# The first layer of chunks 4 to 11 taken in pairs of chunks, as seven block products in place of eight

## The chip, the cores and the metric

The kernel runs on one core of a Trainium2 chip. The metric is the device time of one launch in microseconds, the median over runs. TensorE (PE) multiplies, VectorE (DVE) and ScalarE (ACT) work on its results, GpSimd (POOL) on data outside PSUM, SyncE (SP) issues most transfers.

## What is computed

Attention with a local window, eight global keys and a distance bias, then a two-layer network with a Gelu:

```python
scores = scale * np.matmul(q, k.transpose(0, 1, 3, 2)) + bias
scores = np.where(keep, scores, -1000000000.0)
a = np.exp(scores - np.max(scores, axis=-1, keepdims=True))
a = a / (np.sum(a, axis=-1, keepdims=True) + 1e-09)
x = np.matmul(a, v)            # 4 batches, 8 heads, 768 tokens, 64 -> 3072 tokens x 512
h = x @ w_in                   # 512 -> 2048
g = 0.5 * h * (1.0 + erf(h / np.sqrt(2)))
out = g @ w_out                # 2048 -> 512
```

## The kernel before

The 3072 tokens are cut into 12 chunks of 256 (`CT`). A chunk's attention is taken by head pairs `p` = 0 to 3: `scores_pair` (PE, then a masked maximum on DVE, L373), `exps` (exponentials on ACT, L402; factors on DVE, L404 and L405; scaling on POOL, L411), `flip` (transposes on PE, L423, and a copy on ACT, L427), `av_pair` (products with the values for two head pairs at once, L461; the two partial sums are copied by ACT, L493, and added by DVE, L494; then x is split into two float16 parts, the high one by ACT, L496, the low one by DVE, L191).

Every float32 operand of the network is split into a high and a low float16 part, and a product is three matmuls: high by high, high by low, low by high. The hidden 2048 columns are taken in 8 steps of 256. In a step of a chunk `m1` computes both 128-column halves of the hidden layer (`f` = 0, 1: 12 matmuls of 256 columns each, L537) into one PSUM tile `h`; `gelu` runs the Gelu on ACT (L553) and splits it on DVE (L554, L192); `m2` adds the step to the chunk's two output tiles `acc` (`k` = 0, 1: 6 matmuls of 512 columns each, L581). `send` copies a finished tile on ACT, sends it, and DVE takes its row maxima.

`run` writes the order out by hand as a loop over a time T, one step each: first layer of step T+1, its Gelu, second layer of step T, and between them the pieces of attention that `att` finds due. `START` gives the T at which a chunk's attention begins and `EVENTS` the offsets of its pieces. Chunk c's attention (c at least 3) begins at T = 8c - 7, takes 8 steps, and its scores and exponentials come two head pairs at a time (`EVS`). A compiler then places the instructions, each engine works its own queue in order, and a wait in a queue holds all behind it.

The weights arrive as 64-bit words; they are turned into floats (`split_weights`, L233 to L237) and split (`part_weights`, L247, L192) during the first steps, in which chunks 0 and 1 go side by side. From T = 19 on the words are loaded a second time and compared (`check_load`, `check_words`, L261, 32 pieces of four DVE operations), every second step. `bounds` keeps running maxima and minima of x and of the weights on DVE (L196).

ACT holds one table at a time; between exponentials and Gelus it loads another (ACT_TABLE_LOAD). `self.table` fixes the order of the two kinds.

## Time and profile before

| | |
|---|---|
| median of 3 runs | 647.58 us (647.2 to 648.36) |
| profiled execution | 647.65 us, its span 645.8 us |
| PE busy | 628.7 us, 97% of the span |
| DVE busy | 369.2 us, 57% |
| ACT busy | 313.0 us, 48% |
| POOL busy | 80.4 us, 12% |
| mean granted clock of PE | 0.991 |

The span reaches from the first to the last instruction that the profile shows; the time of the execution is 1.85 us longer. A busy share is an average over stages. Which engine the end hangs on is read stage by stage, from the stretches and from what each waits for. Lengths of operations that follow each other on one engine overlap; the distance of their starts is what one costs.

### The profile page before, as it was taken

What the parts mean: (1) busy time and instruction counts of PE and PEld (TensorE: products, weight loads), DVE (VectorE), ACT (ScalarE), POOL (GpSimd) and SP (SyncE); (2) the same over time, 40 slices, a digit from 0 to 9 for tenths busy, and PEclk for the clock granted to TensorE, in tenths of its full rate; (3) what the DMA queues carried; (4) which work ended last, traced back from release to release, by engine and by line L of the source; (5) the groups of instructions that cost most, each with busy time, mean ns of one, the idle gap of its engine ahead of it and who ended that gap; (6) DMA issues with size and microseconds to landing.
All of it is one profiled execution on the core that took longest, in us unless ns stands there. A gap on an engine that the chain in (4) does not pass through costs nothing.

```text
span 645.8 us, 14522 instructions
## 1 busy us (share of the span) xinstructions
PE 628.7 (97%) x5712; PEld 424.3 (66%) x5712; DVE 369.2 (57%) x1160; ACT 313.0 (48%) x757; POOL 80.4 (12%) x175
## 2 busy tenths in 40 slices
...
GB/s 256 261 177 266 262 73 192 115 37 144 171 24 143 119 56 162 113 37 147 80 94 165 49 124 165 11 138 133 17 172 128 37 172 66 33 2 1 34 1 38
DMA packets 66187, 71.27 MB, mean 110 GB/s; under 512 B 32704, under 2 KB 49344, under 8 KB 66112
## 3 DMA queue, kind: packets, MB, share of 16 engines
...
q14 instruction: 28, 0.23, 0.1%
HBM read 63.97 MB, written 6.29 MB: 109 GB/s over the span
## 4 chain that ended last, share of the span: by engine, by line
PE 84%; DVE 9%; ACT 4%; issue 1%; DMA 1%; POOL 0%; POOLq 0%; ACTq 0%; DVEq 0%
PE h L537 33%; PE acc L581 32%; PE av L461 5%; PE t L423 5%; PE s L362 4%; PE h L531 2%; PE acc L566 2%; DVE wb L235 2%; ACT n L402 1%; DVE wb L237 1%; DVE wb L233 1%; DVE n L373 1%; DVE gl L192 1%; DVE ta L150 1%; DVE winl L192 1%
## 5 line engine op out<-in xcount | busy, mean ns | idle before, releaser
L537 PE MATMUL h<-x,winh 128*128 128x256 f16 x1344 | 228.3, 274 | 0.9 <-ACT x L503 0.4
L537 PE MATMUL h<-x,winl 128*128 128x256 f16 x672 | 184.0, 274 | 0.0
L554 DVE TENSOR_SCALAR gh<-gr 128x512 f16<-128x512 f32 x96 | 42.7, 445 | 213.6 <-ACT gr L553 213.6
L537 PEld LDWEIGHTS <-winh 128*128 128x128 f16 x1344 | 131.5, 98 | 32.9 <-issue 1.4
L411 POOL TENSOR_SCALAR n<-n,su 128x192 f32<-128x192 f32 (+1 forms) x160 | 75.2, 489 | 494.3 <-ACT n L402 240.2
L553 ACT ACTIVATE gr<-h 128x512 f32<-128x512 f32 x96 | 57.3, 597 | 153.9 <-issue 87.3
L581 PE MATMUL acc<-wouth,gl 128*128 128x512 f16 x336 | 127.0, 379 | 1.0 <-DVE gl L192 1.0
L581 PE MATMUL acc<-wouth,gh 128*128 128x512 f16 x336 | 127.5, 380 | 0.1
L581 PE MATMUL acc<-woutl,gh 128*128 128x512 f16 x336 | 127.3, 379 | 0.0
L581 PEld LDWEIGHTS <-gh 128*128 128x128 f16 x672 | 64.2, 98 | 66.0 <-issue 4.3
L427 ACT COPY pt<-t 128x384 f32<-128x384 f32 x96 | 45.1, 475 | 93.7 <-PE t L423 92.0
L537 PEld LDWEIGHTS <-winl 128*128 128x128 f16 x672 | 66.1, 98 | 9.7 <-issue 0.8
L192 DVE SCALAR_TENSOR_TENSOR gl<-gr,gh 128x512 f16<-128x512 f32 x96 | 66.7, 694 | 8.5
L402 ACT ACTIVATE n<-n,mn 128x192 f32<-128x192 f32 (+1 forms) x144 | 62.1, 432 | 4.1 <-DVE mn L373 3.9
L581 PEld LDWEIGHTS <-gl 128*128 128x128 f16 x336 | 32.9, 98 | 41.0 <-DVE gl L192 1.5
L373 DVE CUSTOM_DVE_ANT_0 n<-s,pens 128x192 f32<-128x192 f32 (+1 forms) x192 | 54.9, 341 | 0.1
L423 PE MATMUL t<-ident,n 128*128 128x128 f32 x288 | 47.8, 276 | 3.2 <-DVE n L411 2.4
L461 PE MATMUL av<-pt,vr 64*64 64x64 f32 (+2 forms) x1312 | 42.4, 250 | 2.0 <-ACT pt L427 2.0
L461 PEld LDWEIGHTS av<-pt,vr 64*64 64x64 f32 (+1 forms) x1312 | 35.4, 134 | 11.5 <-issue 8.0
L423 PEld LDWEIGHTS t<-ident,n 128*128 128x128 f32 x288 | 34.7, 142 | 8.5 <-DVE n L411 2.4
L362 PE MATMUL s<-kr,qr 64*64 64x192 f32 (+2 forms) x752 | 39.1, 323 | 0.7 <-DMA kr<-kT 0.7
L261 DVE SCALAR_TENSOR_TENSOR wand<-c,wand 128x128 int32<-128x128 int32 x128 | 37.5, 293 | 2.7
...
## 6 DMA issues: line engine op xcount, KB each, us to landing
...
kr<-kT SPq DMA_DIRECT2D x36, 64.0 KB, 3.3
```

The source lines that it names most:

```text
L192: return self.nc.vector.scalar_tensor_tensor(out=out, in0=in_, scalar=scale, in1=hi, op0=ALU.mult, op1=ALU.subtract)
L362: ins = nc.tensor.matmul(out, lhsT=lhs, rhs=rhs, start=True, stop=True).ins
L373: ins = nc.vector.tensor_tensor_reduce(out=nn[:, j * NK:j * NK + n], in0=sp[hh][:, j, 0:n], in1=self.pens[:, 2 * p + hh, o:o + n], scale=- ...
L402: self.table(nc.scalar.activation(out=nn, in_=nn, func=AF.Exp, bias=mn[:, i:i + 1], scale=-1.0, accum_out=su[:, i:i + 1]))
L411: ins = eng.tensor_scalar(out=nn, in0=nn, scalar1=su[:, i:i + 1], scalar2=0.0, op0=ALU.mult, op1=ALU.add)
L423: self.last_t = nc.tensor.transpose(tp[:, i, :], nn[:, o:o + P], self.ident).ins
L427: ins = nc.scalar.copy(pt, tp).ins
L461: ins = nc.tensor.matmul(out, lhsT=lhs, rhs=rhs, start=start, stop=stop, skip_group_check=True).ins
L537: ins = nc.tensor.matmul(hp[:, f, :], lhsT=w[:, d, fs], rhs=x[:, d, e, :], start=n == 0, stop=n == 3 * NP - 1).ins
L553: self.table(nc.scalar.activation(out=gr, in_=hp, func=AF.Gelu, scale=1.0 / (WS * XS)))
L554: nc.vector.tensor_scalar(out=gh, in0=gr, scalar1=GS, scalar2=None, op0=ALU.mult)
L581: ins = nc.tensor.matmul(acc, lhsT=g[:, f, ks], rhs=w[:, f, :], start=s == 0 and n == 0, stop=(s == NST - 1 or (c, s) == (NCH - 1, NST - 2 ...
```

## The change

Chunks 0 to 3 keep the loop over T, which ends after chunk 3. Chunks 4 to 11 go in four pairs. A **double** `n` (0 to 15, and a 16th pass that only finishes) takes two chunks and two steps, so the first layer is a 2 by 2 block product: weights A (two hidden steps by two halves of the 512 inputs), tokens B (two halves of the inputs by two chunks). It is computed from seven block products P1 to P7 of 12 matmuls each, in place of eight. Four of the weight blocks are replaced by the sums S1 to S4, formed once (`sums`, every second T from 19 on), four of the token blocks by the differences T1 to T4 (`tokens`, once for each pair of chunks). P1, P6, P5 and P3 pile up in one PSUM tile, `hX`; P2, and then P7 and P4, in another, `hW`, which P7 starts anew. In between ACT copies the state after P1, P6 and P7 out, and DVE adds P2, P4 and P5 to the copies. These are three of the four results C11, C21, C22; C12 is what `hX` holds at the end. Each gets its Gelu and split (`gelu2`).

`ORDER` lists what PE does in a double: the seven products, and eight times `m`, a second-layer half (6 matmuls of 512 columns) of the double before. In double 0 there is none before, so its `m` places are empty. A double also has half a chunk's attention, that of chunk 6 + n // 2, until double 11.

The attention of chunks 3, 4 and 5 begins at T = 15, 21 and 27, six steps apart, with a batch of exponentials for each head pair (`EVC`). The check of the weights moves into the doubles, as do the weights' bounds. x is kept in float32 as well (`xf`).

```diff
-START = [-7, -3, 8] + [8 * c - 7 for c in range(3, NCH)]
+START = [-7, -3, 8, 15, 21, 27]
 EVF = {"load": -9, "loadv": -9, "s": (0, 1, 2, 3), "exp": (0, 1, 2, 3), "pt": (2, 3, 4, 5), "av": (2, 3, 4, 5)}
-EVS = {"load": -3, "loadv": 1, "s": (0, 0, 4, 4), "exp": (0, 0, 4, 4), "pt": (2, 3, 6, 7),
-       "av": (4, 4, 8, 8)}
-EVT = {"load": -2, "loadv": 2, "s": (0, 1, 4, 5), "exp": (1, 1, 5, 5), "pt": (3, 4, 7, 8),
-       "av": (5, 5, 9, 9)}
-EVENTS = [EVF, EVF, EVT] + [EVS] * (NCH - 3)
+EVT = {"load": -2, "loadv": 2, "s": (0, 1, 4, 5), "exp": (1, 1, 5, 5), "pt": (3, 4, 7, 8), "av": (5, 5, 9, 9)}
+EVC = {"load": -1, "loadv": 3, "s": (0, 1, 3, 4), "exp": (0, 1, 3, 4), "pt": (2, 3, 5, 6), "av": (4, 4, 7, 7)}
+EVENTS = [EVF, EVF, EVT, EVC, EVC, EVC]
+PAIRED = 4
...
-STEPS += [(c, s) for c in range(2, NCH) for s in range(NST)]
+STEPS += [(c, s) for c in range(2, PAIRED) for s in range(NST)]
+DOUBLES = 4 * (NCH - PAIRED) // 2
+ORDER = ("P1", "m", "P2", "m", "P7", "m", "P6", "m", "P4", "m", "P5", "m", "m", "P3", "m")
+FACTORS = {"P1": ("A11", "B11"), "P2": ("A12", "B21"), "P3": ("S4", "B22"), "P4": ("A22", "T4"), "P5": ("S1", "T1"),
+           "P6": ("S2", "T2"), "P7": ("S3", "T3")}
...
-        a = self.sm.tile([P, 512], I32, name=f"wb{s}_{i}", tag="o", bufs=3)
+        a = self.sw[s][:, i] if i < 2 else self.sm.tile([P, 512], I32, name=f"wb{s}_{i}", tag="o", bufs=3)
...
-            xs = self.sm.tile([P, 2, n, P], F32, name=f"xs{c}_{p}", tag="o", bufs=3)
-            nc.scalar.copy(xs, rows[1])
-            nc.vector.tensor_tensor(out=xs, in0=rows[0], in1=xs, op=ALU.add)
-            xh, xl = (self.x[c][:, ps.start:ps.stop, e].rearrange("d p (j q) -> d j p q", j=2) for e in range(2))
-            nc.scalar.copy(xh, xs)
-            self.lo_dve(xl, xs, xh)
+            xf = self.xf[c % 2][:, ps.start:ps.stop].rearrange("d p (j q) -> d j p q", j=2)
+            t = self.sm.tile([P, 2, n, P], F32, name=f"xs{c}_{p}", tag="o", bufs=3)
+            nc.scalar.copy(t, rows[1])
+            nc.vector.tensor_tensor(out=xf, in0=rows[0], in1=t, op=ALU.add)
+            xh, xl = (self.x[c][:, ps.start:ps.stop, e] for e in range(2))
+            xf = self.xf[c % 2][:, ps.start:ps.stop]
+            nc.scalar.copy(xh, xf)
+            if c < PAIRED or c % 2 == 0 or p == NP - 1:
+                self.lo_dve(xl, xf, xh)
             if p == NP - 1:
-                self.bounds(self.xtop, self.xlow, self.x[c][:, :, 0, :])
+                self.bounds(self.x[c][:, :, 0, :])
...
+    def sums(self, s):
+        nc = self.nc
+        a = self.sw[s].bitcast(F32).rearrange("p i (d f) -> p i d f", d=2)
+        a11, a21, a12, a22 = a[:, 0, :, 0:P], a[:, 0, :, P:], a[:, 1, :, 0:P], a[:, 1, :, P:]
+        t = self.stg.tile([P, 4, 2, P], F32, name=f"sf{s}", tag="stage")
+        for o, x, y, op in ((0, a21, a22, ALU.add), (1, t[:, 0], a11, ALU.subtract), (2, a11, a21, ALU.subtract),
+                            (3, a12, t[:, 1], ALU.subtract)):
+            self.behind(nc.vector.tensor_tensor(out=t[:, o], in0=x, in1=y, op=op))
+        half = self.sw[s].rearrange("p i c -> p (i c)").bitcast(F16).rearrange("p (e c) -> p e c", e=2)
+        flat = t.rearrange("p s d f -> p (s d f)")
+        nc.scalar.activation(out=half[:, 0], in_=flat, func=AF.Copy, scale=WS)
+        self.behind(self.lo_dve(half[:, 1], flat, half[:, 0], WS))
...
+    def tokens(self, c):
+        nc = self.nc
+        xa, xb = self.xf[c % 2], self.xf[(c + 1) % 2]
+        t1 = None
+        for j, x, y in ((2, xb[:, 2:4], xb[:, 0:2]), (0, xb[:, 0:2], xa[:, 0:2]), (1, xb[:, 2:4], 0), (3, xa[:, 2:4], 1)):
+            t = self.sm.tile([P, 2, CT], F32, name=f"xt{c}_{j}", tag="o", bufs=3)
+            nc.vector.tensor_tensor(out=t, in0=x, in1=t1 if isinstance(y, int) else y, op=ALU.subtract)
+            t1 = t
+            nc.scalar.copy(self.xt[:, j, 0], t)
+            self.lo_dve(self.xt[:, j, 1], t, self.xt[:, j, 0])
...
+    def product(self, n, name):
+        nc = self.nc
+        c, u = PAIRED + 2 * (n // 4), n % 4
+        which = "X" if name in ("P1", "P6", "P5", "P3") else "W"
+        start = name in ("P1", "P2", "P7")
+        if name in ("P1", "P2"):
+            self.h[which] = self.bank([P, 2, CT], f"h{which}{n}")
+        out = self.h[which]
+        first = True
+        for i in range(2):
+            (wh, wl), (xh, xl) = (self.factor(f, c, 2 * u + i) for f in FACTORS[name])
+            for d in range(2):
+                for w, x in ((wh, xh), (wh, xl), (wl, xh)):
+                    ins = nc.tensor.matmul(out[:, i], lhsT=w[:, d], rhs=x[:, d], start=start and first,
+                                           stop=i == 1 and d == 1 and w is wl, skip_group_check=True).ins
+                    self.unit(ins, first)
+                    first = False
+        if name in ("P1", "P6", "P7"):
+            self.part[name] = self.cp.tile([P, 2, CT], F32, name=f"{name}_{n}", tag=name)
+            nc.scalar.copy(self.part[name], out)
+        elif name in ("P2", "P4", "P5"):
+            t = self.part[{"P2": "P1", "P4": "P6", "P5": "P7"}[name]]
+            nc.vector.tensor_tensor(out=t, in0=out, in1=t, op=ALU.add)
...
+    def gelu2(self, n, name):
+        nc = self.nc
+        f, j, src = {"C11": (0, 0, "P1"), "C22": (1, 1, "P7"), "C21": (1, 0, "P6"), "C12": (0, 1, None)}[name]
+        gr = self.part[src] if src else self.gp.tile([P, 2, CT], F32, name=f"gr{n}", tag="gr")
+        self.table(nc.scalar.activation(out=gr, in_=gr if src else self.h["X"], func=AF.Gelu, scale=1.0 / (WS * XS)))
+        gh, gl = (self.gp.tile([P, 2, CT], F16, name=f"g{e}{n}_{name}", tag=f"g{e}", bufs=6) for e in "hl")
+        self.behind(nc.vector.tensor_scalar(out=gh, in0=gr, scalar1=GS, scalar2=None, op0=ALU.mult))
+        self.lo_dve(gl, gr, gh, GS)
+        self.g[n, j, f] = gh, gl
...
+    def second(self, n, m):
+        nc = self.nc
+        j, k, i = m // 4, m // 2 % 2, m % 2
+        c, u = PAIRED + 2 * (n // 4) + j, n % 4
+        s = 2 * u + i
+        if s == 0:
+            pool, tag = (self.ps, "ps") if j else (self.ps_acc, "ps_acc")
+            self.acc[c, k] = pool.tile([P, DM], F32, name=f"acc{c}_{k}", tag=tag)
...
+    def pairs(self, flag_i):
+        self.last_unit = None
+        self.part = {}
+        self.cp = self.ctx.enter_context(self.tc.tile_pool(name="cp", bufs=1))
+        for n in range(DOUBLES + 1):
+            c, p = PAIRED + 2 + n // 2, 2 * (n % 2)
+            att = c < NCH
+            if n == DOUBLES:
+                self.flag(flag_i)
+            m = 0
+            for at, name in enumerate(ORDER):
+                if att:
+                    if at in (0, 3):
+                        self.scores_pair(c, p + at // 3)
+                        self.exps(c, p + at // 3)
+                    if at in (6, 7, 9, 10):
+                        self.flip(c, 2 * p + (6, 7, 9, 10).index(at))
+                    if at == 11:
+                        self.av_pair(c, p + 1)
+                if name != "m":
+                    if n < DOUBLES:
+                        self.product(n, name)
+                elif n:
+                    self.second(n - 1, m)
+                    m += 1
+                if n < DOUBLES and at in (5, 9, 11, 13):
+                    self.gelu2(n, {5: "C11", 9: "C21", 11: "C22", 13: "C12"}[at])
+                if att and p and c + 1 < NCH:
+                    if at == 6:
+                        self.load(c + 1)
+                    if at == 13:
+                        self.load_v(c + 1)
+                if n < 16 and at in (1, 8):
+                    self.check_load(2 * n + (at == 8))
+                if n < 16 and at in (8, 14):
+                    self.check_words(2 * n + (at == 14))
+                if 4 <= n < 12 and at == 12:
+                    self.bounds(self.win[n - 4][0])
+            if n % 4 == 3 and n + 1 < DOUBLES:
+                self.tokens(PAIRED + 2 * (n // 4 + 1))
...
-            k = T - 16 - GAP
-            if 0 <= k < 64 and k % 2 == 0:
-                self.check_load(k // 2)
-            if 2 <= k < 66 and k % 2 == 0:
-                self.check_words((k - 2) // 2)
             if T in (15, 16):
-                self.bounds(self.xtop, self.xlow, self.x[T - 15][:, :, 0, :])
-            if 20 <= T < 36 and T % 2 == 0:
-                self.bounds(self.wtop, self.wlow, self.win[(T - 20) // 2][0])
+                self.bounds(self.x[T - 15][:, :, 0, :])
+            if T >= 19 and T % 2:
+                self.sums((T - 19) // 2)
+            if T == 32:
+                self.load(PAIRED + 2)
...
+        self.load_v(PAIRED + 2)
+        self.tokens(PAIRED)
+        self.pairs(flag_i)
```

Three places where rows stand otherwise than before. The first is DVE where the first layer of chunk 4 begins. Before, in a step (this one is of a later chunk, all are alike), Gelu splits follow each other, with a piece of the weight check and the add of an attention sum:

```order
L554 TENSOR_SCALAR gh_4735<-gr_4737 128x512
L192 SCALAR_TENSOR_TENSOR gl_4736<-gr_4737,gh_4735 128x512
L554 TENSOR_SCALAR gh_4789<-gr_4791 128x512
L192 SCALAR_TENSOR_TENSOR gl_4790<-gr_4791,gh_4789 128x512
L261 SCALAR_TENSOR_TENSOR wand<-c_2_4698,wand 128x128 x4
L554 TENSOR_SCALAR gh_4843<-gr_4845 128x512
L192 SCALAR_TENSOR_TENSOR gl_4844<-gr_4845,gh_4843 128x512
L494 TENSOR_TENSOR xs_3_4883<-av_3_0_4849,xs_3_4883 128x512
```

Now, at double 0 (`xt` are the differences T, `P_0` the copy of P1, `s` the scores of chunk 6; ISA is the masked maximum):

```order
L756 TENSOR_REDUCE otop<-o_1_3270 128x1
L377 ISA n_0_3310,mn_0_3298<-s_0_3300,pens 128x128
L377 ISA mn_0_3298 128x1
L377 ISA n_0_3310,mn_0_3298<-s_0_3300,pens 128x192
L377 ISA mn_0_3298 128x1
L377 ISA n_1_3313,mn_0_3298<-s_1_3301,pens 128x128
L377 ISA mn_0_3298 128x1
L377 ISA n_1_3313,mn_0_3298<-s_1_3301,pens 128x192
L377 ISA mn_0_3298 128x1
L616 TENSOR_TENSOR xt_0_3283<-xf_347,xf_346 128x512
L193 TENSOR_TENSOR xt<-xt_2_3279,xt 128x512
L662 TENSOR_TENSOR P_0_3340<-hW_3344,P_0_3340 128x512
```

The add of P2, for which P7 waits, stands behind the row maximum of chunk 3's output, a head pair's four maxima, the difference T1 and the low part of T3.

The second is DVE after a chunk's attention is complete. Before, the attention sum, a head pair's maxima, the low part of x and the bounds:

```order
L494 TENSOR_TENSOR xs_3_4883<-av_3_0_4849,xs_3_4883 128x512
L373 ISA n_0_4902,mn_0_4890<-s_0_4892,pens 128x192
L373 ISA mn_0_4890 128x1
L373 ISA n_0_4902,mn_0_4890<-s_0_4892,pens 128x192
L373 ISA mn_0_4890 128x1
L373 ISA n_1_4905,mn_0_4890<-s_1_4893,pens 128x192
L373 ISA mn_0_4890 128x1
L373 ISA n_1_4905,mn_0_4890<-s_1_4893,pens 128x192
L373 ISA mn_0_4890 128x1
L191 TENSOR_TENSOR x<-xs_3_4883,x 128x2x2x128
L196 TENSOR_TENSOR xtop<-xtop,x 128x1024
L196 TENSOR_TENSOR xlow<-xlow,x 128x1024
```

Now, at double 4, where the pair of chunks changes:

```order
L377 ISA n_0_4485,mn_0_4473<-s_0_4475,pens 128x192
L377 ISA mn_0_4473 128x1
L194 SCALAR_TENSOR_TENSOR gl_C_4437<-gr_4434,gh_C_4436 128x512
L377 ISA n_1_4488,mn_0_4473<-s_1_4476,pens 128x192
L377 ISA mn_0_4473 128x1
L377 ISA n_1_4488,mn_0_4473<-s_1_4476,pens 128x192
L377 ISA mn_0_4473 128x1
L193 TENSOR_TENSOR xt<-xt_3_4469,xt 128x512
L412 TENSOR_TENSOR nmax<-nmax,mn_0_4473 128x4
L408 TENSOR_SCALAR su_0_4474<-su_0_4474 128x4
L409 RECIPROCAL su_0_4474<-su_0_4474 128x4
L662 TENSOR_TENSOR P_4_4515<-hW_4525,P_4_4515 128x512
```

The low part of the last difference and the split of the Gelu of C12 (`gl_C`) stand among the maxima of a head pair; the add of P2 follows four rows after that low part, behind the factors `su`.

The third is ACT in the steps before the pairs, a chunk's two later head pairs. Before, one load for two head pairs:

```order
L402 ACT_TABLE_LOAD
L402 ACTIVATE n_4_2695,su_2_2684<-n_4_2695,mn_2_2683 128x192 x2
L402 ACTIVATE n_5_2698,su_2_2684<-n_5_2698,mn_2_2683 128x192 x2
L402 ACTIVATE n_6_2713,su_3_2702<-n_6_2713,mn_3_2701 128x192 x2
L402 ACTIVATE n_7_2716,su_3_2702<-n_7_2716,mn_3_2701 128x192 x2
L553 ACT_TABLE_LOAD
L553 ACTIVATE gr_2793<-h_2766 128x512
L427 COPY pt_4_2832<-t_4_2828 128x384
L553 ACTIVATE gr_2848<-h_2815 128x512
```

Now a load to and from the exponentials for each, with a weight sum (`sw`) between:

```order
L406 ACT_TABLE_LOAD
L406 ACTIVATE n_4_2399,su_2_2388<-n_4_2399,mn_2_2387 128x192 x2
L406 ACTIVATE n_5_2402,su_2_2388<-n_5_2402,mn_2_2387 128x192 x2
L607 ACTIVATE sw_870<-sf_2428 128x1024
L557 ACT_TABLE_LOAD
L557 ACTIVATE gr_2462<-h_2435 128x512
L499 COPY xs_1_2500<-av_1_1_2467 128x512
L503 CAST x<-xf_346 128x2x256
L406 ACT_TABLE_LOAD
L406 ACTIVATE n_6_2517,su_3_2506<-n_6_2517,mn_3_2505 128x192 x2
L406 ACTIVATE n_7_2520,su_3_2506<-n_7_2520,mn_3_2505 128x192 x2
L431 COPY pt_4_2574<-t_4_2570 128x384
```

Here the Gelu `gr` and the second batch each stand behind a load of their own; in the whole program there are 28 and 27 loads for the two kinds, and before 22 and 21.

## Rows read from the trace of the kernel before

**Rows 1.** The page, part 1: busy us, share of the span, instructions.

```profile
PE 628.7 (97%) x5712; PEld 424.3 (66%) x5712; DVE 369.2 (57%) x1160; ACT 313.0 (48%) x757; POOL 80.4 (12%) x175
```

**Rows 2.** Busy times by stretch: us, busy of each engine, clock, DMA, GB/s.

```profile
140.00:180.00 40.00, 40.00 (x393) 27.52 (x390) 23.93 (x81) 21.98 (x56) 6.94 (x16) 1.00 0.45 143
...
580.00:620.00 40.00, 40.00 (x331) 27.27 (x329) 17.65 (x32) 7.42 (x13) 0.00 (x0) 1.00 0.04 14
```

**Rows 3.** Timeline of PE, 189 to 206 us: start, length, line, operation.

```profile
189.31 1.49 PE L461 MATMUL av<-pt,vr 64*64 64x128 f32 x45
...
192.10 0.39 PE L581 MATMUL acc<-wouth,gh 128*128 128x512 f16 x1
...
199.91 0.38 PE L537 MATMUL h<-x,winh 128*128 128x256 f16 x2
...
201.22 0.49 PE L423 MATMUL t<-ident,n 128*128 128x128 f32 x3
201.55 0.38 PE L537 MATMUL h<-x,winh 128*128 128x256 f16 x2
...
203.18 0.38 PE L581 MATMUL acc<-wouth,gh 128*128 128x512 f16 x1
...
205.77 0.38 PE L537 MATMUL h<-x,winh 128*128 128x256 f16 x2
```

**Rows 4.** Groups of DVE by shape: busy us, mean ns, idle before.

```profile
L261 DVE SCALAR_TENSOR_TENSOR wand<-c,wand 128x128 int32<-128x128 int32 x128 | 37.5, 293 | 2.7
...
L494 DVE TENSOR_TENSOR xs<-av,xs 128x512 f32<-128x512 f32 x18 | 12.4, 689 | 2.9 <-ACT xs L493 2.9
```

**Rows 5.** Timeline of DVE, 192 to 199 us.

```profile
192.60 0.69 DVE L191 TENSOR_TENSOR x<-xs,x 128x512 f16<-128x512 f32 x1 [0.68 <-ACT x L496]
193.21 0.68 DVE L196 TENSOR_TENSOR xtop<-xtop,x 128x1024 f16<-128x1024 f16 x1
...
194.42 0.35 DVE L373 CUSTOM_DVE_ANT_0 n<-s,pens 128x192 f32<-128x192 f32 x1
...
194.69 0.35 DVE L373 CUSTOM_DVE_ANT_0 n<-s,pens 128x192 f32<-128x192 f32 x1
```

**Rows 6.** Groups of ACT by shape.

```profile
L553 ACT ACTIVATE gr<-h 128x512 f32<-128x512 f32 x96 | 57.3, 597 | 153.9 <-issue 87.3 <-PE h L537 62.4 <-PE h L531 4.0
L402 ACT ACTIVATE n<-n,mn 128x192 f32<-128x192 f32 x120 | 52.8, 441 | 2.9 <-DVE mn L373 2.8
L427 ACT COPY pt<-t 128x384 f32<-128x384 f32 x96 | 45.1, 475 | 93.7 <-PE t L423 92.0 <-ACT o L608 1.6
L402 ACT ACT_TABLE_LOAD x22 | 28.2, 1283 | 7.4 <-DMA qr<-qT 7.0
L553 ACT ACT_TABLE_LOAD x21 | 26.9, 1283 | 0.8
...
L493 ACT COPY xs<-av 128x512 f32<-128x512 f32 x18 | 10.5, 586 | 13.1 <-PE av L461 13.1
```

**Rows 7.** Groups of POOL by shape.

```profile
L411 POOL TENSOR_SCALAR n<-n,su 128x192 f32<-128x192 f32 x136 | 66.9, 507 | 366.1 <-ACT n L402 240.2 <-DVE su L405 101.1 <-DVE mx L698 21.8
```

**Rows 8.** Busy times by stretch of 2 us, 48 to 56 us.

```profile
48.00:50.00 2.00, 0.23 (x2) 0.14 (x2) 1.90 (x7) 2.00 (x7) 0.00 (x0) 1.00 0.00 0
50.00:52.00 2.00, 2.00 (x16) 1.28 (x16) 2.00 (x6) 2.00 (x5) 0.00 (x0) 0.72 0.91 285
52.00:54.00 2.00, 2.00 (x11) 1.56 (x10) 2.00 (x5) 0.67 (x3) 0.00 (x0) 0.50 1.02 334
54.00:56.00 2.00, 2.00 (x47) 1.35 (x46) 1.02 (x2) 1.97 (x4) 0.00 (x0) 0.93 1.20 323
```

**Rows 9.** DMA: KB and median us to landing, then the queue's timeline at 167 us.

```profile
kr<-kT SPq DMA_DIRECT2D x36, 64.0 KB, 3.3
...
167.22 0.38 SPq L299 DMA_DIRECT2D qr<-qT  x1
167.71 5.18 SPq L299 DMA_DIRECT2D kr<-kT  x8
```

107 lines of the change are left out of this document (66 added, 41 removed).

## The prediction

> **What bounds the kernel now.** I read the page first, then the busy times by stretch, then the order of TensorE's work in a step. TensorE (PE) is busy 97% of the span, VectorE (DVE) 57%, ScalarE (ACT) 48% [rows 1]. From 140 us to 620 us PE is busy in all of each 40 us stretch; twelve stretches, of which the first and the last stand in [rows 2]. There PE's own work is the time, and a matmul taken away is time gained, if nothing else comes to make PE wait. The price is read from starts, since the recorded lengths overlap: twelve first-layer matmuls run from 199.91 to 201.22, so 1.31 us or 109 ns each; three transposes take 0.33; twelve second-layer matmuls run from 203.18 to 205.77, 2.59 us [rows 3]. A step (24 and 12 matmuls) is 5.21 us. A half of a chunk's attention costs PE 2.79 (value products 1.39, scores of two head pairs 0.7 each) [rows 3] and four groups of transposes of 0.33.
>
> **What is removed.** A double replaces 4 steps: 8 blocks of 12 matmuls become 7. Over 16 doubles 192 matmuls go, at 109 ns: **21.0 us**. Nothing else leaves PE; all attention and the second layer are only moved.
>
> **What is added off PE.** In a double ACT gets three copies out of PSUM and DVE three adds. The nearest rows are the copy of an attention sum, 0.59, and its add, 0.69 [rows 4, 6]. DVE's lengths overlap too: the 128x512 low part of x, 0.69 long, holds its queue for 0.61 from its start to the next one's, a masked maximum, 0.35 long, for 0.27 [rows 5]; I take 0.60 and 0.28 for queues. A double with attention lasts 4 x 5.21 - 1.31 + 4.1, so about 23.7 us. ACT's share of it is three copies, four Gelus at 0.60, eight exponentials at 0.44, four probability copies at 0.48, two passes of an attention block and two table loads at 1.28 [rows 6], 13.4 in all; DVE's, counted in the same way, is about 14. Both fit. So the cost lies only where PE comes to a block before what it waits for. I played the queues of the new program by hand against these starts; four places matter.
>
> (1) **A usual double.** P7 restarts the bank that P2 filled, so it waits for DVE to add P2. Between the two stand scores (0.7) and one second-layer half (1.30): 2.0 us of cover against 0.7 to 0.8 for the add and its start, 1.2 spare. The add stands behind the scale factors of the head pair, and these behind its exponentials; the exponentials end some 3.8 us after the double begins and P2 at 4.7, so the add isn't late. P4 needs ACT's copy of P7: P7 ends at 8.0, ahead of the copy are four exponentials, a load and a Gelu, it is done at 10.2, and PE comes at 12.6. P5 needs the copy of P6, 11.5 against 15.9; P3 the add of P5, 18.1 against 21.2. No wait: 0.
>
> (2) **The first double** has no second layer between its blocks, and the token differences T1 to T4 of its own chunks are formed in it. Count from the last value product of chunk 5. PE does the second layer (2.6), scores, P1, P2, scores, and stands at P7 at 6.7. DVE gets the attention sum at 0.7, waits for ACT's rounding until 2.7, and then works without a pause: the low part, two bounds, T3, a row maximum, four score maxima, T1, T3's low part, P2's add: 8 x 0.60 + 4 x 0.28 + 0.09, done at 8.7. PE waits 2.0. Twelve entries later comes T2's low part, at 13.0, and the first transposes need the factors that stand just ahead of it and then GpSimd, 0.5 for each operation [rows 7]: P6 waits 3.0. P4 waits 0.9 for ACT, which has two table loads and seven exponentials on the way to T4, and then 0.35 for its low part; a transpose 0.65. Together 6.9, and the next double, whose exponentials start late, waits 0.9 for its transposes: **7.8**. With the full lengths (0.69 in place of 0.60) the same count gives 9.6; half of it if the queues stand closer.
>
> (3) **The three later changes of pair.** The differences of the next pair stand in DVE's queue ahead of P2's add. From the add of P5 on, 17.35 after the double's start, come the two Gelu splits, the attention sum, four differences, four low parts, two bounds and four maxima. In the fifth double the add also stands behind the scale factors, whose exponentials wait for ACT to finish the differences and load a table (29.0); it ends at 32.1, PE is there at 30.5: 1.6. In the ninth, with two more bounds but ahead of the factors, 31.3: 0.9. In the thirteenth there is no attention, so only 1.3 of cover, and ten operations of the weight check at 0.29 [rows 4] crowd the queue: 32.1 against 29.0, 3.1. Together **5.6**; with full lengths 10.4.
>
> (4) **TensorE's clock.** In 48 to 50 us PE ran 0.23 of 2 us, and in the next 6 us the granted share was 0.72, 0.50 and 0.93, half speed being the 1.2 GHz level [rows 8]: 0.56 + 1.0 + 0.14, about 1.7 us of PE time lost. The wait ahead of P6 and the one in the thirteenth double are as long. I take one such fall, **1.7**, with 0 and 3.4 as bounds.
>
> **The steps before the pairs** get one more chunk's attention (moved, not added), eight weight sums and twelve more table loads (28 + 27 in place of 22 + 21). A chunk's attention now lies on six steps, for PE 6 x 5.21 + 8.2 = 39.5. ACT has four batches of exponentials with two loads each, 4 x (2 x 1.28 + 4 x 0.44) = 17.3, eight probability copies 3.8, two attention blocks 2.4, six Gelus 3.6, three sums of 1024 at most 1.2 each, 3.6, and an output, 0.8: 31.5 of 39.5. A Gelu can come 1.7 late after a load; its user comes 5.5 later and the chain to it takes 1.8. DVE has less: a sum is four adds of 256 and a split of 1024, under four and two times the 0.69 of 512 [rows 4], some 3 us in two steps. I take 0.5, up to 3, for all of it. Chunk 4's keys now have two steps (11 us and more) where three lay before; its issues took from 167.2 to 172.9 and a landing of such a piece 3.3 [rows 9], 9 in all, so 0. The tail is as it was.
>
> **The sum.** -21.0 + 7.8 + 5.6 + 1.7 + 0.5 = -5.4. The profiled execution took 647.65 (span 645.8, 1.85 around it), 0.07 above the median, 647.58. **Forecast: 642.2 us.**
>
> **Two banks for seven blocks.** In [rows 3] a block starts where the second layer ends, with no wait for an eviction; there each step has a PSUM tile of its own. The seven blocks share two tiles. If each of the five reuses in a double were exposed for a copy or add and its start, about 0.65, that would cost 16 x 3.3 = 52 us, less 21: 679. Against it stands that between a block and its tile's reuse lie 2.0 us or more of other matmuls, apart from the first and the last doubles, where the adds still fit into 1.3. The Trainium skill, Perfetto Trace Analysis, section Optimizing Tensor Performance, speaks against this change: independent groups of matmuls should rotate through different PSUM banks, so that one's eviction overlaps the next. By that rule it would be the 679, by the rows 642.2; no row of before shows a tile reused so soon.
>
> **Rivals.**
> *The queues keep up better* (what DVE waits for comes earlier than in my count; half of (2) and (3), no clock fall): 647.6 - 21.0 + 6.7 = 633. For it: DVE was idle for over a third of the span [rows 1]. Against it: in (2) the count has hardly a pause in it.
> *The usual double waits too: slower.* Its 1.2 us of cover ahead of P7 is used up, because the exponentials that stand ahead of P2's add start late: on ACT they come behind the last Gelu of the double before and a table load of 1.28. Each us beyond the 1.2 costs a us in each of eleven doubles. From 0.5 us on average (5.4 / 11) it is no faster than before; at 1.0 it gives 653. For it: ACT's queue has loads of 1.28 that can slip; against it: spare on three chains.
> *The gain is eaten without a single cause* (first double at its full lengths, two clock falls, 3 in the steps before): 642.2 + 1.8 + 1.7 + 2.5 = 648, no change. It is also what would be seen if the words of the weight check, loaded behind v, came late in the first double, since the check stands ahead of later sums on DVE.
> *Every reuse of the two banks exposed*: 679, by the reasons above the least likely.
>
> **How the numbers follow.** Forecast 0.55, better queues 0.17, the late exponentials 0.15, no change 0.10, every reuse exposed 0.03. 0.2% is 1.3 us, about what a measurement of this kernel can tell from no change: faster 0.72, same 0.10, slower 0.18. The range runs from just under the second case, 632, to the slower one at half a us to one per double, 652.
>
> **What would show it.** In the profile of after: PE's first-layer matmuls 192 fewer; PE full in the usual doubles, with no wait for DVE ahead of P7; two or three PE waits of 1 to 3 us in the first double, behind DVE's low parts and GpSimd; one of about 1 to 3 ahead of P7 in the fifth, ninth and thirteenth; the clock share down once. It is wrong if PE waits in every double, if the steps before chunk 4 get longer by more than one chunk's attention, or if the first double takes under 18 or over 27 us from the last value product of chunk 5.

## The result and the profile after

The changed kernel takes **656.62 us** (median of 4 runs, 656.35 to 657.81). Its time is 1.014 of that of the kernel before (95% interval 1.0123 to 1.0158): 1.4% slower, where 642.2 was forecast and 632 to 652 given as range. The profiled execution took 656.35, its span is 654.5 (645.8 before).

From the page, the busy times (us, share, instructions) and the stores (issues, KB each, median us to landing):

```profile
PE 625.7 (96%) x5520; PEld 406.9 (62%) x5520; DVE 432.4 (66%) x1276; ACT 371.9 (57%) x841; POOL 84.2 (13%) x173
...
out<-o ACTq DMA_DIRECT2D x23, 256.0 KB, 2.0
```

The 192 matmuls are gone (5520 in place of 5712), but PE is busy only 3 us less than in [rows 1]: what is left takes longer, so the busy time tells little. I measured each double, from the start of its P1 to the start of the next one's. The starts of doubles 2 and 3 in the timeline of PE:

```profile
305.40 0.39 PE L653 MATMUL hX<-x,winh 128*128 128x256 f16 x2
...
328.86 0.88 PE L366 MATMUL s<-kr,qr 64*64 64x192 f32 x16
329.68 0.39 PE L653 MATMUL hX<-x,winh 128*128 128x256 f16 x2
```

A usual double lasts 305.40 to 329.68, 24.3 us (24.1 to 24.3 in eight of them, 24.2 on average), a double without attention 19.5; no wait of PE stands between 282 and 350 us. Four doubles are longer, those that begin a pair of chunks: 0 (23.2, without second layer, so 13.8 of its own), 4 (26.6), 8 (26.7) and 12 (27.6 in place of 19.5). The balance against the kernel before, in us:

| | forecast | measured | from |
|---|---|---|---|
| eighth product left out, 16 doubles | -21.0 | -20.6 | 19.55 for a double without attention, 4 x 5.21 before |
| attention in usual doubles | 0 | +6.0 | 12 x (24.2 - 23.7) |
| doubles 0 and 1 | +7.8, clock 1.7 | +9.4, 0 in double 1 | 23.2 - 13.8 |
| doubles 4, 8, 12 | +1.6, +0.9, +3.1 | +2.4, +2.5, +8.1 | over 24.2, 24.2, 19.5 |
| steps before the pairs | +0.5 | +2.9 | double 0 begins at 258.1; the same work was done at 255.2 before |
| the end, behind the last second-layer matmul | 0 | -1.4 | 7.3 before, 5.9 now |

The 255.2 is worked out: the second layer of chunk 4's first step began at 253.46 before. The changed kernel has not done two first-layer steps of it (5.2) at 258.1, but has done three more blocks of scores (2.1), value products twice (2.8) and six more groups of transposes (2.0). The 23.7 fits the kernel before as well: there four steps with half a chunk's attention take 25.0 on average, less 1.31 for a block.

The table sums to 9.3. From it goes one head pair's scores, 0.8, which the usual doubles count and double 11 hasn't (it lasts 23.5): 8.5, and the spans differ by 8.7; 0.2 is not placed.

**Double 0.** The timeline of PE:

```profile
260.81 0.77 PE L366 MATMUL s<-kr,qr 64*64 64x128 f32 x16
263.58 2.69 PE L653 MATMUL hW<-xt,sw 128*128 128x256 f16 x12 [2.00 <-DVE P L662]
267.36 0.37 PE L653 MATMUL hX<-xt,sw 128*128 128x256 f16 x1 [1.08 <-ACT xt L618]
269.85 1.09 PE L427 MATMUL t<-ident,n 128*128 128x128 f32 x3 [2.12 <-POOL n L415]
```

The timeline of DVE in the same stretch:

```profile
262.85 0.69 DVE L662 TENSOR_TENSOR P<-hW,P 128x512 f32<-128x512 f32 x1
...
265.96 0.69 DVE L616 TENSOR_TENSOR xt<-xf,xt 128x512 f32<-128x512 f32 x1 [1.67 <-issue]
...
266.92 0.28 DVE L265 SCALAR_TENSOR_TENSOR wand<-c,wand 128x128 int32<-128x128 int32 x1
...
268.33 0.17 DVE L409 RECIPROCAL su<-su 128x4 f32<-128x4 f32 x1
```

The DMA issues between 250 and 270 us (count, KB each, median us to landing):

```profile
c<-w SPq DMA_DIRECT2D x3, 512.0 KB, 8.6
...
out<-o ACTq DMA_DIRECT2D x2, 256.0 KB, 6.2
```

P7 waits 2.0 for P2's add, as counted. But the third difference, T2, stands 1.7 us at the head of DVE's queue, released by no engine. Its buffer is one that outputs use too (`own_ring` below takes that away), and the two stores of chunk 3 take 6.2 us to land in place of 2.0 (page), beside 512 KB pieces of the weight check and smaller ones of v. By the trace the second store, issued at 258.12, landed at 265.88; T2 starts at 265.96. Comparisons stand between what follows, the factors of the transposes among it (268.33).

**Double 12.** The queue of SP from 480 us on:

```profile
497.96 3.03 SPq L303 DMA_DIRECT2D vr<-v  x6
501.09 48.26 SPq L204 DMA_DIRECT2D c<-w  x12
```

The timeline of DVE, 541 to 567 us:

```profile
543.09 0.94 DVE L265 SCALAR_TENSOR_TENSOR wand<-c,wand 128x128 int32<-128x128 int32 x3 [1.02 <-DMA c<-w]
543.95 0.68 DVE L662 TENSOR_TENSOR P<-hW,P 128x512 f32<-128x512 f32 x1
...
551.84 0.62 DVE L265 SCALAR_TENSOR_TENSOR wand<-c,wand 128x128 int32<-128x128 int32 x2 [0.86 <-DMA c<-w]
552.38 0.68 DVE L500 TENSOR_TENSOR xf<-av,xs 128x512 f32<-128x512 f32 x1
...
561.94 0.68 DVE L662 TENSOR_TENSOR P<-hW,P 128x512 f32<-128x512 f32 x1
```

The waits of PE, 540 to 580 us (us in total, times, longest):

```profile
PE hW L653 <- DVE P L662: 5.5, 1, 5.5
```

From 501 us on the last twelve loads of the check follow one another, as fast as their three buffers come free, and DVE compares whatever has landed. In DVE's order 34 of the 128 comparisons stand between the start of double 11 and the attention sum `xf`, where the program lists eight for a double. DVE waits at them for words that are still on the way (1.02 and 0.86), the attention sum begins at 552.38, 5.5 us after the value products end (1.0 in `no_check` below), and P2's add at 561.94: PE waits 5.5.

**Doubles 4 and 8** have the waits that were forecast, for P2's add, and one for scores. The waits of PE, 350 to 380 us:

```profile
PE hW L653 <- DVE P L662: 1.3, 1, 1.3
```

And 450 to 470 us:

```profile
PE hW L653 <- DVE P L662: 0.9, 1, 0.9
PE s L366 <- DVE mn L377: 0.4, 1, 0.4
```

These waits are 1.3 in each of the two, of the 2.4 and 2.5 that the doubles are longer. The rest is no wait that the profile shows and no fall of the clock. Part of it: the compiler cut the value products of both in two, 4 and 60 matmuls with second-layer matmuls between, and the scores of double 4 in 2 and 14. What such a cut costs is measured below.

**The clock** fell twice, in doubles 0 and 12 (busy times by stretch; the granted share stands before the last two columns, and 0.50 is the 1.2 GHz level):

```profile
262.00:264.00 2.00, 0.41 (x3) 0.31 (x3) 2.00 (x7) 1.99 (x9) 0.00 (x0) 0.91 0.98 384
264.00:266.00 2.00, 2.00 (x11) 1.44 (x10) 0.34 (x5) 1.85 (x9) 0.00 (x0) 0.50 0.55 216
...
270.00:272.00 2.00, 2.00 (x9) 1.37 (x10) 1.70 (x5) 1.17 (x3) 2.00 (x4) 0.50 0.00 0
560.00:562.00 2.00, 0.00 (x0) 0.00 (x0) 2.00 (x6) 1.11 (x2) 0.00 (x0) 0.65 0.01 4
562.00:564.00 2.00, 1.32 (x7) 0.95 (x7) 2.00 (x6) 0.63 (x1) 0.00 (x0) 0.50 0.37 139
```

### The profile page after: what moved, and what is told of

Its sections match the earlier page's. It is cut to its first block, busy times and chain, and to the rows that moved or that the text cites. A ratio compares the mean times of both kernels' runs of the same rounds, so it can differ in the third digit from the quotient of the medians.

```text
span 654.5 us, 14272 instructions
## 1 busy us (share of the span) xinstructions
PE 625.7 (96%) x5520; PEld 406.9 (62%) x5520; DVE 432.4 (66%) x1276; ACT 371.9 (57%) x841; POOL 84.2 (13%) x173
## 4 chain that ended last, share of the span: by engine, by line
PE 69%; DVE 13%; DMA 6%; ACT 5%; SPq 4%; issue 2%; POOL 0%; DVEq 0%; ACTq 0%; POOLq 0%
PE acc L688 20%; PE hX L653 11%; PE hW L653 8%; PE acc L585 8%; PE h L541 7%; SPq L303 4%; PE s L366 4%; PE av L466 4%; PE t L427 3%; DMA c<-w 3%; PE acc L570 3%; PE h L535 2%; DMA kr<-kT 2%; ACT n L406 2%; DVE xt L616 1%
## 5 line engine op out<-in xcount | busy, mean ns | idle before, releaser
L688 PE MATMUL acc<-wouth,gh_C 128*128 128x512 f16 x256 | 97.7, 382 | 0.0
L688 PE MATMUL acc<-woutl,gh_C 128*128 128x512 f16 x256 | 97.6, 381 | 0.0
L688 PE MATMUL acc<-wouth,gl_C 128*128 128x512 f16 x256 | 97.3, 380 | 0.0
L653 PEld LDWEIGHTS <-sw 128*128 128x128 f16 x768 | 76.7, 100 | 29.1 <-issue 11.2
L688 PEld LDWEIGHTS <-gh_C 128*128 128x128 f16 x512 | 48.7, 98 | 40.7 <-issue 3.7
L541 PE MATMUL h<-x,winh 128*128 128x256 f16 x320 | 55.2, 274 | 1.5 <-ACT x L511 1.4
L653 PE MATMUL hX<-xt,sw 128*128 128x256 f16 x384 | 49.1, 277 | 1.1 <-ACT xt L618 1.1
L653 PEld LDWEIGHTS <-winh 128*128 128x128 f16 x384 | 36.7, 98 | 14.8 <-issue 3.3
L466 PE MATMUL av<-pt,vr 64*64 64x128 f32 (+2 forms) x1312 | 44.3, 250 | 1.6 <-ACT pt L431 1.6
L688 PEld LDWEIGHTS <-gl_C 128*128 128x128 f16 x256 | 25.2, 98 | 30.0 <-issue 0.6
L541 PE MATMUL h<-x,winl 128*128 128x256 f16 x160 | 43.8, 274 | 0.0
```

The source lines that it names most:

```text
L466: ins = nc.tensor.matmul(out, lhsT=lhs, rhs=rhs, start=start, stop=stop, skip_group_check=True).ins
L541: ins = nc.tensor.matmul(hp[:, f, :], lhsT=w[:, d, fs], rhs=x[:, d, e, :], start=n == 0, stop=n == 3 * NP - 1).ins
L653: ins = nc.tensor.matmul(out[:, i], lhsT=w[:, d], rhs=x[:, d], start=start and first, stop=i == 1 and d == 1 and w is wl, skip_group_check ...
L688: ins = nc.tensor.matmul(acc, lhsT=g, rhs=w[:, f, :], start=s == 0 and q == 0, stop=q == 5 and s in (NST - 3, NST - 1), skip_group_check=T ...
```

## The experiments

Sixteen runs, each beside the kernel before on the same chip (medians 648.05 to 648.19; 647.72 beside the changed kernel). Doubles 0, 4, 8, 12 are from the profiled execution, us:

| run | median us | ratio (95%) | 0 | 4 | 8 | 12 |
|---|---|---|---|---|---|---|
| changed kernel | 656.62 | 1.0140 (1.0123 to 1.0158) | 23.2 | 26.6 | 26.7 | 27.6 |
| no_check | 641.77 | 0.9900 (0.9882 to 0.9918) | 20.0 | 25.0 | 24.6 | 19.8 |
| no_loads | 648.86 | 1.0034 (1.0007 to 1.0061) | 20.9 | 25.5 | 25.0 | 23.2 |
| own_ring | 653.77 | 1.0102 (1.0049 to 1.0155) | 19.4 | 25.0 | 29.4 | 27.1 |
| fill | 658.03 | 1.0139 (1.0097 to 1.0181) | 25.1 | 26.9 | 25.7 | 25.4 |
| pin_alone | 648.53 | 1.0008 (0.9986 to 1.0030) | 23.3 | 25.2 | 25.1 | 20.4 |
| check_spread | 649.54 | 1.0042 (1.0009 to 1.0074) | 18.9 | 24.8 | 26.1 | 27.0 |
| pinned | 644.58 | 0.9969 (0.9939 to 0.9999) | 18.9 | 25.9 | 26.0 | 21.0 |
| queue | 643.71 | 0.9945 (0.9912 to 0.9979) | 18.9 | 24.8 | 25.0 | 21.6 |
| queue_cover | 643.56 | 0.9959 (0.9924 to 0.9995) | 18.9 | 25.3 | 25.3 | 21.4 |
| queue_early | 641.96 | 0.9915 (0.9891 to 0.9938) | 16.8 | 25.3 | 25.3 | 21.4 |
| early_cover | 647.87 | 0.9989 (0.9964 to 1.0013) | 16.9 | 25.3 | 25.6 | 21.5 |
| pinned_early | 644.49 | 0.9948 (0.9921 to 0.9975) | 16.8 | 25.4 | 26.1 | 19.7 |
| pinned_pairs | 655.26 | 1.0101 (1.0058 to 1.0145) | 17.0 | 25.9 | 25.9 | 19.7 |
| av_next_to_scores | 658.96 | 1.0185 (1.0123 to 1.0248) | 24.5 | 25.9 | 27.7 | 28.1 |
| before_split | 653.22 | 1.0073 (1.0051 to 1.0095) | | | | |
| before_av_apart | 652.97 | 1.0075 (1.0051 to 1.0098) | | | | |

The single runs of most versions of the changed kernel scatter by 6 to 9 us. In the profiles double 0 begins at 258 to 260 us, but at 264.5 in `fill`, whose edit touches nothing there. The traces show where that comes from: the first scaling of chunk 2's exponentials on GpSimd. In the changed kernel, in the timeline of POOL:

```profile
96.88 0.91 POOL L415 TENSOR_SCALAR n<-n,su 128x192 f32<-128x192 f32 x1 [92.70 <-DVE su L409]
```

And in `fill`:

```profile
99.23 4.33 POOL L416 TENSOR_SCALAR n<-n,su 128x192 f32<-128x192 f32 x1 [95.05 <-DVE su L410]
```

It takes 4.33 in place of 0.91, PE waits 3.0 for the transposes behind it, and the granted clock is 0.50 in 106 to 108 us. Why the same operation takes so long there is open. So the doubles are compared one by one.

**The weight check.**

```
no_check: -  self.check_load(...)  -  self.check_words(...)    # both left out of the doubles
no_loads: -  w = self.raw.pop((n, "chk"))
          +  w = self.sw[0] ...        # words that lie in SBUF, result into a tile of its own
```

> The changed kernel without the second loading and the comparison of the weight words in the doubles (left out, 32 pieces; the flag then says nothing of them). Theory W (the words come late: their loads crowd the stores and the loads in double 0, and DVE stands at a comparison for words that have not landed ahead of double 12): the wait ahead of P7 in double 12 falls from 5.5 to 2 or less and TensorE's clock keeps its level there (another 2.4), the second wait of double 0 (1.1 for the low clock's P6 and 2.1 for GpSimd) falls by about 1.5; together 6 to 8, 649 to 651. Rival (the queue is long by itself, the words only fill gaps): only the ten comparisons of 0.29 ahead of the add in double 12 go, 3 us at most, 653.5 to 656.

> The changed kernel with all 128 comparisons in their places, but of words that lie in SBUF already, into a tile of their own: the second loading of the weights in the doubles is left out, and nothing is checked. Without loads and comparisons the time was 641.8. Theory W (the loads do the damage: they delay stores and hold DVE at words that have not landed): most of the 14.8 us comes back, the comparisons alone leave 1 to 4 at the changes of pair: 643 to 646. Rival V (DVE's own time does it, 128 comparisons of 0.3 are 38 us ahead of other things): 651 to 657.

Without the check the kernel takes 641.77, 14.9 less and twice what was expected, and the four doubles together are 14.7 shorter. The whole loss against the forecast has about this size, but it is not the check's alone (the last part comes back to this). In double 0 T2 then follows P2's add at once, as the timeline of DVE of `no_check` shows:

```profile
263.27 0.69 DVE L662 TENSOR_TENSOR P<-hW,P 128x512 f32<-128x512 f32 x1
...
263.94 0.68 DVE L616 TENSOR_TENSOR xt<-xf,xt 128x512 f32<-128x512 f32 x1
...
267.40 0.17 DVE L409 RECIPROCAL su<-su 128x4 f32<-128x4 f32 x1
```

And the clock keeps its level, in the busy times of `no_check` by stretch:

```profile
262.00:264.00 2.00, 0.25 (x8) 0.10 (x1) 2.00 (x7) 1.99 (x6) 0.00 (x0) 1.00 0.00 0
...
266.00:268.00 2.00, 0.59 (x6) 0.41 (x5) 1.64 (x6) 1.98 (x10) 0.23 (x1) 1.00 0.00 0
```

Comparisons without loads leave 5.2 of the 14.7 (0.9, 0.5, 0.4 and 3.4); loads and late words make the other 9.5. Both theories have a part; in the doubles the loads have the larger one. By the medians the split is even (7.1 and 7.8): the profiled execution of `no_loads` was the fastest of ten. In double 12 the comparisons alone still make PE wait, in the waits of PE of `no_loads`, 545 to 575 us:

```profile
PE hW L655 <- DVE P L664: 3.5, 1, 3.5
```

That is near the 3.1 that was forecast for double 12. And the clock keeps its level beside this wait, in the busy times of `no_loads` by stretch:

```profile
552.00:554.00 2.00, 0.00 (x0) 0.00 (x0) 2.00 (x6) 0.72 (x2) 0.00 (x0) 1.00 0.01 4
```

**A buffer of its own for T.**

```
-  name=f"xt{c}_{j}", tag="o", bufs=3
+  name=f"xt{c}_{j}", tag="xt", bufs=2
```

> The changed kernel with the token differences in two buffers of their own; before they took turns with the outputs and the attention sums in three. In double 0 the third difference, T2, stood 1.7 us on DVE with no engine named as its releaser, and went on when the stores of chunk 3, slow beside the loads, were through. Theory R (it waits for the buffer of a store): double 0 gets 1.5 to 3 us shorter (23.2 to some 21), the rest as it was: 654 to 655. Rival (it waits for something else, or what follows is late anyway): double 0 within 0.5 us of 23.2, 656.6.

Double 0 is 3.8 shorter, more than expected: the wait was for the buffer of a store. Double 8 got 2.7 longer, with a wait of 2.3 for P2's add in place of 0.9 and a fall of the clock to 0.50 that the changed kernel didn't have; why its queue stood otherwise was not tested.

**Filling the waits.**

```
+  self.fill(18 ahead of P7, 20 ahead of P6 in double 0; 45 ahead of P7 in double 12)
```

> The changed kernel with idle transposes of the identity (0.109 each) where TensorE waits: 18 ahead of P7 and 20 ahead of P6 in double 0, 45 ahead of P7 in double 12, about as long as the waits (2.0, 2.2 and 4.9 of 5.5). They add work and take no wait away; they keep TensorE occupied. Theory C (the clock that falls in the waits costs as much as the waits): in double 0 some 35 matmuls ran at 0.21 in place of 0.109, in double 12 about 20 and six of 0.43 in place of 0.216, so 3.2 and 2.4 us come back: 651 to 652. Rival (the half speed lies on no path, since DVE and GpSimd set the end of these stretches anyway): 0 to 1 us, 655.6 to 657.

Missed. Double 12 got 2.2 shorter, about what the clock was said to cost there, but double 0 got 1.9 longer. There the compiler set the first transpose ahead of the 20 fillers, so they stood behind the wait and not in it: PE waited 5.0 for GpSimd, and the fillers took 3.7 behind that. So the clock's price could be had back in double 12, and double 0 doesn't test it.

**Where the check stands.**

```
pin_alone:    +  self.after(ins, self.last_unit, ...)      # loads and comparisons, not ahead of their place
check_spread: check only in doubles with n % 4 > 0, compared two loads later; T in own buffers
pinned:       check_spread + pin_alone
```

> The changed kernel with one thing added: the loads and the comparisons of the weight check may not be placed ahead of the matmuls behind which the program lists them. In the changed kernel the compiler drew the last loads together (12 behind each other on SyncE, 501 to 549 us) and put 34 of the 128 comparisons into double 11 and 7 more ahead of P2's add in double 12; now each double has its two pieces, and double 12 three comparisons ahead of that add. Theory B (the bunch at doubles 11 and 12, and three loads at once in double 0, make the damage): double 12 from 27.6 to 21 or 22, doubles 0 and 8 by about 1 each, together 648 to 649. Rival (loads or comparisons do harm wherever they are): 653 or more.

> The changed kernel with the differences in buffers of their own and with the weight check only in the doubles that don't begin a pair of chunks, up to three pieces in each, every piece compared two loads after its own load. All work is there. Theory W: the words are landed when they are compared and nothing of them stands at a change of pair, so nearly the time without the check, 641.8: 641 to 644. Rival V: the comparisons fill DVE in the usual doubles and make these wait, more than 646.

> The one with the check in doubles that begin no pair, with the same pins added. As it stood, the compiler had again drawn 34 comparisons into double 11 and one into double 12, which took 27.0 us. Theory B: doubles 4, 8 and 12 as without the check (25.0, 24.6, 19.8), double 0 near 19: 640 to 642. Rival: double 12 stays at 25 or more, 647 and up.

`pin_alone` changes nothing but the place and gives 8.1 us back. In its profile double 12 is 7.2 shorter, doubles 4 and 8 are 1.4 and 1.6 shorter, and the part from double 15 on is 1.4 longer, since comparisons now stand there. (The expectation miscounts: behind the 34, four comparisons stood ahead of that add in the changed kernel and two behind it.) Its last twelve loads now spread over 98.7 us, in its queue of SP:

```profile
499.79 98.70 SPq L204 DMA_DIRECT2D c<-w  x12
```

The wait for that add is 0.7, in its waits of PE, 540 to 575 us:

```profile
PE hW L656 <- DVE P L665: 0.7, 1, 0.7
```

Double 0 stayed, so the expected 1 there was wrong. `check_spread` shows the reverse: the program lists no check in double 12, but the compiler drew 36 comparisons into double 11, and double 12 takes 27.0; its time is over 646, as rival V had it, but no usual double waits. With both, `pinned` has 21.0 there, and its median is 2.6 above the expected 642: pieces at the end of doubles 3, 7 and 11 still stand ahead of the changes (four comparisons ahead of the attention sum in double 11).

**What is left at the changes.**

```
queue:       fewer pieces ahead of a change, bounds of the weights in doubles 13 to 15
queue_cover: + COVER = ("P1","m","P2","m","m","m","P7","P6",...) in doubles 4, 8, 12
queue_early: + START = [..., 15, 20, 26], chunk 3 in seven steps
early_cover, pinned_early: START = [-7, -3, 7, 14, 20, 26], COVER, on check_spread and on pinned
```

> The spread and pinned check, with still less ahead of the changes of pair: one or two pieces in the doubles before a change in place of three, four in the last three doubles, and the bounds of the weights moved from doubles 4 to 11 to doubles 13 to 15. Theory D (what is left at doubles 4, 8 and 12 is DVE's queue): double 4 from 25.9 to 25, double 8 from 26.0 to 24.8, double 12 from 21.0 to 20; 3 less, 641 to 642. Rival: within 1 us of 644.6.

> The one before with three second-layer halves ahead of P7 in doubles 4, 8 and 12 in place of one, 2.6 us more cover. If what is left there is a wait for P2's add of under 2.6, doubles 4 and 8 come to 24.2 and 12 to 19.6: 639.5 to 641. If it is another wait (transposes, T2 and T4 behind ACT), no gain: 641 to 642.5.

> The one before with the attention of chunks 4 and 5 one step earlier, and that of chunk 3 squeezed for it into seven steps, chunk 2 as it was. With chunk 2 moved too, double 0 fell from 18.9 to 16.9 but began 4 to 6 us later. If that delay came from chunk 2's place among the splitting of the weights: double 0 at 16.9, begun at 258 as before, 637.5 to 639. If it comes from any earlier attention: begun at 261 or later, 641 or more.

> The one before, and besides: the attention of chunks 2 to 5 one step earlier, and in doubles 4, 8 and 12 three second-layer halves ahead of P7 in place of one. Without the check double 0 took 20.0 us where its matmuls take 13.9, and doubles 4 and 8 had 0.8 and 0.4 more than a usual one. Theory Q (what is left there are DVE's queue and GpSimd behind the last attention): with 5.2 us more ahead of double 0 some 4 to 6 come back, and about 1 at the changes: 635 to 639. Rival (the early steps pay for it, since the attention of chunk 2 now stands in the steps in which the weights are split): no better than the one before, 641 to 645.

> The one before with the attention of chunks 2 to 5 one step earlier and three second-layer halves ahead of P7 in doubles 4, 8 and 12. In the run with both but with the bunched check double 0 took 16.9 us, and the start of double 0 came 6 us later than elsewhere; the run with fillers showed the same 6 us with no change ahead of the pairs, so I take them for a scatter of the steps before. Theory Q: 2 to 3 less than without, 637 to 640. Rival (the earlier attention costs these 6 us): 643 to 646.

`queue` brings doubles 4 and 8 to 24.8 and 25.0 as expected, not double 12, and its time is within 1 us of `pinned`, as the rival had it. DVE's order shows why: the bounds of the weights, which the program now lists in doubles 13 to 15, hold nothing back either, and the compiler drew them into double 12. Five stand ahead of P2's add there, two in `pinned`. More cover gains nothing: in double 12 the wait of P7 for an add only goes over to another product. The waits of PE in `queue` there:

```profile
PE hW L661 <- DVE P L670: 1.9, 1, 1.9
```

And in `queue_cover`:

```profile
PE hX L662 <- DVE P L671: 1.7, 1, 1.7
```

Earlier attention shortens double 0 to 16.8 or 16.9 in each of the three. Where chunk 2 was moved too, double 0 began at 262.1 to 264.8, so that gain was paid ahead of it: `pinned_early` has 644.49 where `pinned` has 644.58, and `early_cover` missed its 635 to 639 by 9. `queue_early` leaves chunk 2 and has the best median of those with all work there, **641.96, 0.8% faster than the kernel before**; 637.5 to 639 was expected. Its profiled execution, 646.3, is one with a late start of double 0 (263.8), with the same long scaling on GpSimd (4.33) as in `fill`, so its start doesn't decide between the two expectations.

**The attention's small matmuls.**

```
before_split:      -  "s": (0, 0, 4, 4), "exp": (0, 0, 4, 4)    +  "s": (0, 1, 4, 5), "exp": (1, 1, 5, 5)
                   +  self.after(ins, self.last_m1[1], ...)     # scores not ahead of the first layer before them
before_av_apart:   -  "av": (4, 4, 8, 8)                        +  "av": (5, 5, 9, 9)
av_next_to_scores: av_pair at the end of its double (on the changed kernel)
pinned_pairs:      scores of both head pairs at the head of the double (on pinned_early)
```

> The kernel before, with the scores of a chunk's second and fourth head pair one step later (from chunk 3 on, exponentials still in two batches), so that a half of the attention has two score blocks, one of them alone, where it had one double block behind the value products. Not a matmul more or fewer. Theory S (a block of the small float32 matmuls costs more for each place at which it is entered): in the changed kernel a usual double takes 24.17 us where 23.68 was counted, with two more entries; 0.25 for each. Here there are 18 more entries (two for each of nine chunks): 18 x 0.25 = 4.5, so about 652 us, with no new wait of PE. Rival Q (the 0.5 of a usual double comes from something else in the doubles, TensorE's work is the same wherever it stands): within 0.7 us of the kernel before, 647.6.

> The kernel before, with the value products one step later from chunk 3 on, so that they stand alone and the scores of two head pairs stand by themselves; the rest as it was. Theory S (each entry into the small float32 matmuls costs 0.25 to 0.28): 18 more entries, 4.5 to 5 us, 652.7 to 653.2. Rival (in the run with the scores apart something else cost 5 us, such as a second pair of table loads or later exponentials): 647.5 to 649.

> The changed kernel, with the value products of a half of the attention put at the end of their double, right ahead of the scores of the next one; not in the doubles before a change of pair. One entry into the small float32 matmuls less in nine doubles. Theory S: 9 x 0.25 = 2.3 us less, 654.4. Rival Q: no gain, 656.6, or some slower, since the sums of the attention come 4 us later.

> The one before with the scores of both head pairs of a half taken together at the head of the double. One entry into the small float32 matmuls less in each of twelve doubles. Theory S: 12 x 0.25, 3 us less than the one before, 634 to 637. Rival (four score banks and the two of the products and two outputs don't fit eight banks without waits): no gain or slower, 638 to 645.

Both edits of the kernel before add 18 places by the program and no matmul (17 in the traces, 58 blocks of these matmuls where the kernel before has 41), and both cost 5 us (653.22 and 652.97 against 648.11 and 648.05). PE's waits don't account for it: between 105 and 634 us they sum to 0.4 before, 0.5 and 1.0 here. `before_av_apart` leaves the exponentials as they were, so they aren't the cause either. It leaves out an order that the result needs: a chunk's first step reads x ahead of its last value products. It stands here for its time alone. The timeline of PE of the kernel before:

```profile
339.36 1.49 PE L461 MATMUL av<-pt,vr 64*64 64x128 f32 x45
...
340.75 1.47 PE L362 MATMUL s<-kr,qr 64*64 64x192 f32 x30
342.15 0.39 PE L581 MATMUL acc<-wouth,gh 128*128 128x512 f16 x1
```

The same of `before_split`:

```profile
342.06 1.49 PE L463 MATMUL av<-pt,vr 64*64 64x128 f32 x45
...
343.44 0.82 PE L362 MATMUL s<-kr,qr 64*64 64x192 f32 x14
344.19 0.39 PE L583 MATMUL acc<-wouth,gh 128*128 128x512 f16 x1
...
349.51 0.88 PE L362 MATMUL s<-kr,qr 64*64 64x192 f32 x16
350.32 0.39 PE L583 MATMUL acc<-wouth,gh 128*128 128x512 f16 x1
```

The same of `before_av_apart`:

```profile
341.99 1.53 PE L362 MATMUL s<-kr,qr 64*64 64x192 f32 x32
343.45 0.39 PE L581 MATMUL acc<-wouth,gh 128*128 128x512 f16 x1
...
348.76 1.55 PE L461 MATMUL av<-pt,vr 64*64 64x128 f32 x48
350.25 0.39 PE L581 MATMUL acc<-wouth,gh 128*128 128x512 f16 x1
```

From start to start: together, value products and 32 score matmuls take 2.79 (339.36 to 342.15). With 16 of them apart, the rest takes 2.13 and the 16 alone 0.81; with the value products apart, these take 1.49 and the 32 scores 1.46. In both the block ahead of the new place ends 0.09 later (24 first-layer matmuls take 2.71 in place of 2.62). So a place costs 0.24 or 0.25 here, and 5 us over 17 places are 0.29 or 0.30.

In a usual double of the changed kernel all three blocks stand alone. The value products there:

```profile
322.06 1.57 PE L466 MATMUL av<-pt,vr 64*64 64x128 f32 x64
323.56 0.39 PE L688 MATMUL acc<-wouth,gh_C 128*128 128x512 f16 x1
```

The two attempts to have it back in the doubles failed. In `av_next_to_scores` the products and scores are neighbours in nine doubles, but mix in only three of them (0.26 saved); in the other six they follow each other (1.39 and 0.88 in one, 0.13 saved). The sums come later, and the doubles as a whole are no shorter. In `pinned_pairs` the usual doubles have 24.1 to 26.7. Its two blocks of scores run without a pause, but the P1 behind them then waits for the maxima of the scores on DVE, as the rival had it. In its waits of PE:

```profile
PE hX L658 <- DVE mn L382: 9.3, 8, 2.6
```

That is most of the 10.8 us that it is slower than `pinned_early`. That the price can be saved in the pairs is not shown.

## Why the prediction was wrong

- **What is removed**: right. 20.6 us of 21.0 are in the doubles.
- **(1) A usual double**: its queues were read rightly, no wait of PE in it. Its length was not: "all attention and the second layer are only moved" priced the moved blocks at nothing. The 2.79 of [rows 3] is the price of value products and two score blocks that stand together, and was split into 1.39 and twice 0.7 as if each had it alone. With what they add to the block ahead, they cost 2.88 together, and 1.59 and twice 0.9 alone, so 0.5 for each double: 6.0. The steps before the pairs, where chunks 3 to 5 are spread in the same way, have seven to ten more places by the timeline of PE, 1.8 to 2.5 of their 2.9 at 0.25 each (an estimate). `before_split` and `before_av_apart` show the price; this term, set at nothing, is some 8 us. It is the first step that failed.
- **(2) The first double**: 8.6 with its clock fall, and 9.4 measured. The first wait was right to a tenth (2.0). The size of the second (3.0, measured 1.1 and 2.1) was right by chance: it was put down to the queues of DVE and GpSimd, and in part it was T2's buffer, behind a slow store; without check or with an own buffer double 0 is 3.2 and 3.8 shorter. The 0.9 in double 1 didn't come.
- **(3) The changes of pair**: mechanism and place right in doubles 4 and 8 (waits of 1.3 and 0.9 for P2's add, 1.6 and 0.9 forecast); the other 1.1 and 1.6 are in part matmuls of the attention in more places, term (1) again. In double 12 the second step failed, "ten operations of the weight check at 0.29 [rows 4] crowd the queue", 3.1: the comparisons were priced as if their words had landed. That price was right for the comparisons alone (a wait of 3.5 in `no_loads`). But loads that nothing holds back had been drawn together, so words were late, the attention sum began 5.5 us after the value products in place of 1.0, and PE waited 5.5, with a clock fall behind it that I had not put there: 4.4 us more than in `no_loads`. `pin_alone`, which moves both back, makes double 12 7.2 shorter.
- **(4) The clock**: two falls, at the two longest waits, for one forecast. `fill` gave 2.2 back in double 12; in double 0 its fillers missed the wait.
- **The steps before and the end**: put at 0.5, up to 3, and at nothing; 2.9 and -1.4 were measured.
- **The rivals**: usual doubles that wait, the rival that forecast slower, did not occur, and neither did the reuse of two banks. The Trainium skill (Perfetto Trace Analysis, Optimizing Tensor Performance) says that independent matmul groups should rotate through different PSUM banks, so that the eviction of one overlaps the matmuls of the next. Here five reuses in each usual double cost PE nothing (no wait between 282 and 350 us), since other matmuls lie between. "The gain is eaten without a single cause" came nearest, and named the check's words, but at double 0 and with 0.10.
- **The range** ended at 652 because two costs had no upper bound in it: the check's loads, which the sum doesn't price, and the moved blocks.

Without the check the time is 641.8, near the forecast of 642.2, but not for its reasons: 8 us of moved attention stand against changes of pair (doubles 0, 4, 8 and 12) that cost 7.7 there in place of the 15.1 forecast with the clock and double 1.
